# Opening of the first attention layer: projections as pairs of 64-row matmuls, and another order of norms, mask copies and late copies

## The chip, the cores and the metric

The kernel runs on one core of one Trainium2 chip. A core has TensorE (PE; matmuls into PSUM, eight banks of 128 x 512 f32), VectorE (DVE), ScalarE (ACT), GpSimd (POOL) and SyncE (SP); DMAs are issued from the queues of SP, ACT and POOL. The metric is the device time of the whole program in microseconds, the median of several executions.

## The reference

Four layers over `x` of 2048 tokens by 576, each with a layer norm ahead and a residual: attention, gated MLP, attention, gated MLP.

```python
def _A_ref(x, wqkv, wo):            # H = 32 heads of Dh = 18, window W = 8, dilation 2
    q, k, v = split(x @ wqkv)
    idx = pos[:, None] - 2 * arange(8)[None, :]     # eight tokens back, two apart
    logits = einsum('bhsd,bhswd->bhsw', q, k[idx]) * Dh ** -0.5   # masked where idx < 0
    return einsum('bhsw,bhswd->bhsd', softmax(logits), v[idx]) @ wo

def _B_ref(x, w_in, w_sp, b_sp, w_out):
    z = gelu(x @ w_in)
    z1, z2 = z[..., :Fh], layernorm(z[..., Fh:])
    return (z1 * (w_sp @ z2 + b_sp)) @ w_out
x = x + _A_ref(layernorm(x)); x = x + _B_ref(layernorm(x)); and both once more
```

## The kernel before

**Data.** In the attention layers the tokens are held with even ones first and odd ones behind (`rows_of`), so that the window is eight neighbours. `xnT` holds the normed input transposed: five chunks of 128 rows by 2048 columns (tokens). The model width of 576 is four full chunks and one of 64 rows; chunk 4 has 64 real rows in partitions 0 to 63. Each 128-token tile `xn` is 640 wide before it is transposed, so partitions 64 to 127 of chunk 4 hold its columns 576 to 639. In layer 0 of the kernel before these are zeros, written once by POOL (L151); in the later layers they are a second copy of columns 512 to 575, and the MLP layers use them.

**Weights.** `wqk` holds chunks 0 to 3 of the Q and K weights, `wqk4` chunk 4. In layer 0 `wqk4` has the weights in partitions 0 to 63 and zeros in 64 to 127 (`zero_right`, L340, on VectorE), so a matmul over all 128 rows of chunk 4 takes the 64 real ones.

**First attention layer (`layer_A`, `li == 0`).** An order written by hand holds for all five engines: each executes its instructions in the order of the program text, and waits where an operand, a buffer or a bank is not ready.

- *Norms.* For each tile of 128 tokens: `B_` (two statistics, L715), `G_` (aggregation, L718), `S_` is both; `R_` adds the epsilon on VectorE (L727) and takes the power -0.5 on POOL (L728); `A_` writes the normed tile (L735, VectorE). The first four tiles are transposed by TensorE (`T_pe`, L742) and copied by ScalarE (L745); the later ones by DMA transposes issued on SP (`T_`, L306). Four buffers of `xn` rotate.
- *V.* `VW(t, hh)` (L451): five matmuls of 288 columns for one query tile (17 tiles of 120 tokens with a halo of 8) and half of the heads, copied out of PSUM into `v_ext` by VectorE or ScalarE (`evac`).
- *Q and K projections.* `PG(d, qk, cc)` (matmuls at L462): one unit is 128 output columns (`d` 0 to 4; `qk` 1 is K, 0 is Q; `d` 4 has the last 64 columns of both in one unit) by 512 tokens (`cc`), five matmuls into one bank, then one copy into a staging tile. When a staging tile of `d` is full, DMAs move its heads' rows into `QK` (L78), on POOL's and SP's queues by turns. The first half (`cc` 0 and 1, 18 units) stands in the opening; six units of `cc` 2 and two more stand ahead of the steps (`pre`), the rest in the steps.
- *Window mask.* The window is added through extra rows of Q and K: `QK` holds 18 rows of data and 14 rows of a fixed pattern for each head. `build_window_rows` makes the pattern: `rows[2]` (VectorE, and two DMAs on SP) and `rows[3]` (POOL, four small instructions and a DMA, L179 to L182 and L78) write one period to DRAM, `load_pat` reads it into `win_pat` with four DMAs on SP, and `fill_window_rows` (L201, L204, VectorE) copies it over a half of `QK`, head groups 0 to 3 and then 4 to 7. The moves of a `d` into `QK` come after the copy over the same groups.
- *Banks.* One tile `X0` of three banks, tag Y with two banks and tag PT with three. `PT_tile` takes the next of the list `ring` ("Y", "Y", "PT", "PT", "PT").
- *Steps.* 34 steps follow, two for each query tile: logits of step s+1 (`L_mm`, L536), exponentials on ScalarE (`EXP`, L545), products with V (`PV`, L559) and what the table `at` puts into the step: projections, V units, transposes of the output `O_T` (L595, copied to `oT` by `evac`), output projection `WO` (L629). `pe_turn` lists the tiles whose output TensorE transposes, among the last 13 and 14 (of 17).

**64-row pairs.** The MLP layers split the rows of a contraction over two tiles of the array of 64 rows by 128 columns, which work side by side on different banks. `mm_phase` (L234) issues, for each chunk, a matmul of each of two outputs on different halves of the rows; then, in a second phase, each output takes the other half of the rows. Between the phases an engine writes a one-element token (`turn_on`), so that the two row tiles take turns on a bank. `pair` keeps two such pairs in flight.

The order in the opening of the kernel before, after the first four tiles:

```python
            S_(4, 5)
            R_(4, 2)
            A_(4, 5)
            T_(4, 5)
            S_(6, 7)
            R_(6, 2)
            rows[3](nc.gpsimd)
            A_(6, 7)
            T_(6, 7)
            S_(8)
            self.load_pat(nc.sync)
            S_(9, 10, 11)
            R_(8, 4)
            S_(12)
            A_(8, 9, 10, 11)
            T_(8, 9, 10, 11)
            self.fill_window_rows(QK, 0)
            S_(13, 14, 15)
```

The 18 units follow, `d` by `d` within `cc`, all copied out by ScalarE, with `R_(12, 4)` on POOL's queue behind the moves of `d` 0 to 2; then V tiles 4 to 7, `A_` and `T_` of tiles 12 to 15, `pre`, V tile 8 and the steps.

## Time and profile before

| | us |
|---|---|
| median of 3 runs | 1155.64 (1155.06 to 1156.4) |
| the profiled execution, its own time | 1155.03 |
| its span | 1153.3 |
| TensorE busy | 1144.1 |
| VectorE, ScalarE, POOL busy | 536.6, 373.3, 259.8 |
| granted TensorE clock, mean | 0.999 |

The first attention layer takes the first 123 us of the span, and the part that the change touches most lies between 1 and 50 us.

How to read the lines: a timeline row is the start in us, the length in us, the engine, the line of the kernel, the operation, output<-inputs, the number of instructions merged, and in brackets the idle time ahead with what ended it; "128*128 128x512" is the stationary and the moving operand of a matmul. SPq and POOLq are the queues on which DMAs are issued; the length there is that of issuing, not of landing. A row of a DMA group ends with its size and the time from issue to landing. A row of a table of windows has the window, its length, the busy time and the number of instructions of PE, PEld, DVE, ACT and POOL, the granted clock, the DMA engines' share and GB/s. The groups of one line give the shortest, the middle and the longest duration in ns.

### The profile page before, as it was taken

What the parts mean: (1) busy time and instruction counts of PE and PEld (TensorE: products, weight loads), DVE (VectorE), ACT (ScalarE), POOL (GpSimd) and SP (SyncE); (2) the same over time, 40 slices, a digit from 0 to 9 for tenths busy, and PEclk for the clock granted to TensorE, in tenths of its full rate; (3) what the DMA queues carried; (4) which work ended last, traced back from release to release, by engine and by line L of the source; (5) the groups of instructions that cost most, each with busy time, mean ns of one, the idle gap of its engine ahead of it and who ended that gap; (6) DMA issues with size and microseconds to landing.
All of it is one profiled execution on the core that took longest, in us unless ns stands there. A gap on an engine that the chain in (4) does not pass through costs nothing.

```text
span 1153.3 us, 29700 instructions
## 1 busy us (share of the span) xinstructions
PE 1144.1 (99%) x12935; PEld 613.6 (53%) x12954; DVE 536.6 (47%) x1189; ACT 373.3 (32%) x669; POOL 259.8 (23%) x387
## 2 busy tenths in 40 slices
PE   9999999999999999999999999999999999999998
PEld 5567554444444444457755774444444444444676
DVE  8788887222233222234476889843322223222311
ACT  5589565011111111102247876641111111011000
POOL 3689655000000000001153776530000000000000
PEclk9999999999999999999999999999999999999999
DMA  8867697000000000049455868930000000000322
GB/s 193 182 162 194 131 204 148 18 13 13 13 1 13 13 13 2 1 140 224 109 110 110 165 167 171 237 73 1 13 13 13 13 12 1 13 2 27 103 74 58
DMA packets 176701, 91.10 MB, mean 79 GB/s; under 512 B 128116, under 2 KB 169748, under 8 KB 176570
## 3 DMA queue, kind: packets, MB, share of 16 engines
q1 hardware_dynamic: 164090, 70.58, 28.0%
q0 software_dynamic: 5888, 12.72, 4.3%
q10 hardware_dynamic: 6592, 5.90, 1.7%
q8 instruction: 101, 1.65, 0.6%
q14 instruction: 30, 0.25, 0.1%
HBM read 35.46 MB, written 14.69 MB: 43 GB/s over the span
## 4 chain that ended last, share of the span: by engine, by line
PE 96%; ACT 1%; DMA 1%; issue 1%; SPq 0%; DVE 0%; DVEq 0%; ACTq 0%
PE hh L234 79%; PE pp L462 6%; PE pv L451 3%; PE pw L629 3%; PE O_ps L559 2%; PE L_ps L536 2%; ACT P_sb L545 1%; DMA wqk_sb<-in_A_wqkv_dram 1%; PE L_ps L462 1%; SPq L78 0%; PE hh L1191 0%; PE pt L595 0%; DVE x_new L632 0%; DVE ln_st L640 0%; ACT v_ext L445 0%
## 5 line engine op out<-in xcount | busy, mean ns | idle before, releaser
L234 PE MATMUL hh<-Wq,Z 64*128 64x512 bf16 x4608 | 505.8, 376 | 0.0
L234 PEld LDWEIGHTS <-Z 64*128 64x128 bf16 x6984 | 338.5, 94 | 311.4
L1095 DVE TENSOR_TENSOR g_tmp<-hh,ln_xn 128x512 f32<-128x512 f32 x144 | 92.8, 686 | 452.3 <-PE hh L234 452.3
L947 ACT COPY bank_turn<-ones 1x1 bf16<-1x1 bf16 x239 | 44.7, 187 | 538.6 <-PE hh L234 534.1
L78 POOL DMA_DIRECT2D wout<-in_B_w_out_dram x4 | 4.3, 1075 | 602.0 <-PE hh L234 602.0
L234 PE MATMUL hh<-wout,Z 64*128 64x288 bf16 x2232 | 137.0, 283 | 0.0
L545 ACT ACTIVATE P_sb<-L_ps 128x1440 bf16<-128x1440 f32 (+3 forms) x136 | 125.1, 972 | 21.8 <-PE L_ps L536 20.6
L234 PE MATMUL hh<-xnT,w 64*128 64x512 bf16 x1152 | 132.1, 376 | 0.0
L234 PE MATMUL hh<-win2a,xnT 64*128 64x512 bf16 (+1 forms) x960 | 118.6, 355 | 0.0
L234 PEld LDWEIGHTS <-xnT 64*128 64x128 bf16 x1440 | 69.6, 94 | 70.3 <-issue 0.5
L1020 DVE BATCH_NORM_STATS2 z_st<-zp 128x6 f32<-128x512 bf16 (+1 forms) x160 | 92.6, 623 | 11.1 <-ACT zp L1018 11.1
L1086 ACT ACTIVATE z1T<-hh 128x1024 bf16<-128x1024 f32 x72 | 73.7, 1024 | 62.2 <-PE hh L234 62.2
L1096 DVE TENSOR_TENSOR Z<-g_tmp,z1T 128x512 bf16<-128x512 f32 x144 | 92.4, 683 | 0.0
L234 PEld LDWEIGHTS <-w 64*128 64x128 bf16 x1152 | 55.8, 94 | 68.5
L1018 ACT ACTIVATE zp<-hh 128x1024 bf16<-128x1024 f32 (+1 forms) x96 | 76.1, 810 | 48.8 <-PE hh L234 48.7
L462 PE MATMUL pp<-xnT,wqk_sb 128*128 128x512 bf16 (+1 forms) x313 | 74.4, 379 | 1.0 <-DMA wqk_sb<-in_A_wqkv_dram 0.2
L234 PE MATMUL hh<-win2b,xnT 64*128 64x512 bf16 (+1 forms) x480 | 72.8, 355 | 0.0
L1160 DVE TENSOR_TENSOR x_new<-hh,xo 128x288 bf16<-128x288 f32 x64 | 26.3, 453 | 92.6 <-PE hh L234 84.7
L299 POOL TENSOR_SCALAR ln_xn<-x_new,ln_mv,ln_rstd 128x576 bf16<-128x576 bf16 x28 | 64.2, 2293 | 2.6
L78 POOL DMA_DIRECT2D QK<-stg x76 | 48.1, 636 | 35.6 <-DVE stg L443 22.5
L1044 POOL TENSOR_SCALAR Z<-zp,z_mv,z_rstd 128x256 bf16<-128x256 bf16 x32 | 51.2, 1599 | 3.5
L462 PEld LDWEIGHTS <-wqk_sb 128*128 128x128 bf16 (+1 forms) x360 | 32.0, 97 | 37.0 <-issue 1.9
(124 smaller groups left out, 755.2 us busy)
## 6 DMA issues: line engine op xcount, KB each, us to landing
xres<-x_new SPq DMA_DIRECT2D x44, 144.0 KB
wout<-in_B_w_out_dram POOLq DMA_DIRECT2D x4, 1296.0 KB, 7.5
xo<-xres SPq DMA_DIRECT2D x32, 144.0 KB
xn_rows<-ln_xn SPq DMA_DIRECT2D x28, 160.0 KB
w<-in_B_w_in_dram SPq DMA_DIRECT2D x16, 256.0 KB
QK<-stg POOLq DMA_DIRECT2D x51, 72.0 KB, 4.4
QK<-stg SPq DMA_DIRECT2D x37, 72.0 KB
xo<-in_A_x_dram SPq DMA_DIRECT2D x6, 288.0 KB
```

The lines of the kernel that those rows point to most:

```text
L78: return eng.dma_start(out=out, in_=in_)
L234: ins = self.nc.tensor.matmul(outs[a_], lhsT=lhs(a_, c, r0), rhs=rhs(a_, c, r0), start=start and k_ == 0, stop=stop and k_ == len(chunks) ...
L299: e.tensor_scalar(out=xn[:nrows, 0:D], in0=x_t[:nrows, :], scalar1=mv[:nrows, 0:1], scalar2=rstd[:nrows, 0:1], op0=ALU.subtract, op1=ALU.mult)
L462: nc.tensor.matmul(pp, lhsT=w, rhs=self.xnT[r0:r1, c, cc * 512:(cc + 1) * 512], start=start, stop=stop, tile_position=(r0, 0))
L545: nc.scalar.activation(out=P_bufs[2 * jp + s % 2][:nk, :, :, 0:nq], in_=Lv[:nk, :, :, 0:nq], func=ACT.Exp, scale=scale)
L947: self.turn_on = lambda tok: nc.scalar.copy(out=tok, in_=self.ones[0:1, 0:1])
L1018: nc.scalar.activation(out=zp[:, w0:w0 + n], in_=pz, func=ACT.Gelu_apprx_tanh)
L1020: nc.vector.bn_stats(out=st[:, x // 512, :], in_=zp[:, x:x + min(512, w0 + n - x)])
L1044: eng.tensor_scalar(out=Z[:, b0:b1, i, :], in0=zv[:, b0:b1, :], scalar1=mv[:, 0:1], scalar2=rstd[:, 0:1], op0=ALU.subtract, op1=ALU.mult)
L1086: lambda ht, z1T=z1T, q2=q2: nc.scalar.activation(out=z1T[:, q2 * 512:(q2 + 2) * 512], in_=ht[:].rearrange("p a b -> p (a b)"), func=ACT.G ...
L1095: nc.vector.tensor_tensor(out=tmp[:], in0=pg[:, a_, :], in1=bsp[:, qs], op=ALU.add)
L1096: nc.vector.tensor_tensor(out=uT(jj)[:, sub, qs], in0=tmp[:], in1=z1Ts[jj, sub][:, qs], op=ALU.mult)
```

## The change

- The 18 projection units become nine pairs, each run by `mm_phase` in two phases of 64-row matmuls: chunks 0 to 3, then the other half of the rows and chunk 4 of both. The first phase of a pair comes ahead of the second phase of the pair before it. ScalarE writes the token. Pairs are K of `d` 0 and 1, K of 2 and 3, Q of both for tokens 0 to 511, then K and Q of each `d` for tokens 512 to 1023, then `d` 4 for both token ranges. Banks go through `X0`, Y and PT in a cycle of four pairs.
- For the 64-row phases chunk 4 needs real data in partitions 64 to 127: `A_` copies columns 512 to 575 again behind each norm (VectorE), POOL's zero padding is gone, and `wqk4` is loaded into partitions 64 to 127 by three DMAs on POOL. VectorE no longer zeroes them at the start but after the last pair.
- Order: `rows[3]` moves ahead of the statistics of tile 4; `S_(6)` and `S_(8)` move ahead of the norms of tiles 4 and 6; the first half of the mask copy moves ahead of the statistics of tiles 9 to 12, the second behind the norms of tiles 8 to 11; the transposes of tiles 8 to 11 move between the pairs; `R_(12, 4)` moves behind the pairs.
- V tile 4 is computed around the last pair, tiles 5 to 8 behind the pairs, tile 9 ahead of the steps; it was tiles 4 to 7 and 8. Steps 10 and 14 lose a V unit each.
- The copies of the transposed output of tiles 13 and 14, and the V copies of steps 27 and 30, go from ScalarE to VectorE.

```diff
-        for xb in self.xn_bufs:
-            nc.gpsimd.memset(xb[:, D:640], 0.0)
...
-    def fill_window_rows(self, QK, half):
+    def fill_window_rows(self, QK, half, g0s=(0, 4)):
...
+    def load_wqk4_again(self, eng):
+        for c0, n, w0 in self.WQK_PARTS:
+            self.dma(self.right["wqk4"][64:128, w0:w0 + n], self.A_wqkv[512:576, c0:c0 + n], eng=eng)
...
-                evac(oT[:, :, c0:c0 + n], pt[:, :, a:a + n], t in pe_turn and t < NT - 4)
+                evac(oT[:, :, c0:c0 + n], pt[:, :, a:a + n], t in pe_turn)
...
-            self.zero_right()
+            self.zero_right(False)
...
+                    nc.vector.tensor_copy(out=xn[:, D:640], in_=xn[:, 512:D])
...
             VW(2, 1, False)
+            rows[3](nc.gpsimd)
+            self.load_wqk4_again(nc.gpsimd)
             VW(3, 0, False)
...
             S_(4, 5)
             R_(4, 2)
+            S_(6)
             A_(4, 5)
             T_(4, 5)
-            S_(6, 7)
+            S_(7)
             R_(6, 2)
-            rows[3](nc.gpsimd)
+            S_(8)
             A_(6, 7)
             T_(6, 7)
-            S_(8)
             self.load_pat(nc.sync)
+            self.fill_window_rows(QK, 0, (0,))
             S_(9, 10, 11)
             R_(8, 4)
             S_(12)
             A_(8, 9, 10, 11)
-            T_(8, 9, 10, 11)
-            self.fill_window_rows(QK, 0)
+            self.fill_window_rows(QK, 0, (4,))
             S_(13, 14, 15)
-            order = [(d, cc) for cc in range(2) for d in range(5)]
-            for k_, (d, cc) in enumerate(order):
-                for qk in ((1, 0) if d < 4 else (0,)):
-                    PG(d, qk, cc, False, (nc.gpsimd, nc.sync) if d in (0, 3, 4) else q2)
-                if k_ == 7:
-                    R_(12, 4)
-            nvw0, nvw = 4, 9
+
+            self.turn_on = lambda tok: nc.scalar.copy(out=tok, in_=self.ones[0:1, 0:1])
+
+            def PG_first(units, outs):
+                def lhs(a_, c, r0):
+                    d, qk, cc = units[a_]
+                    w0 = d * P + (640 if qk else 0)
+                    return wqk[r0:r0 + 64, c, w0:w0 + P] if c < 4 else wqk4[r0:r0 + 64, w0:w0 + P]
+
+                def rhs(a_, c, r0):
+                    cc = units[a_][2]
+                    return self.xnT[r0:r0 + 64, c, cc * 512:(cc + 1) * 512]
+                turn = self.mm_phase(outs, lhs, rhs, [0, 1, 2, 3], 0, True, False)
+
+                def second():
+                    self.mm_phase(outs, lhs, rhs, [0, 1, 2, 3, 4], 1, False, True, turn)
+                    for u, o in zip(units, outs):
+                        PG(*u, False, (nc.gpsimd, nc.sync) if u[0] in (0, 3, 4) else q2, pp=o)
+                return second
+
+            def pair_banks(p):
+                if p % 4 == 0:
+                    return [X0[:, 0, :], X0[:, 1, :]]
+                one = [X0[:, 2, :]] if p % 4 == 2 else []
+                self.ring = ["Y"] if p % 4 == 1 else ["PT"]
+                return one + [self.PT_tile([P, 512], f32, "pp")[:, :] for _ in range(2 - len(one))]
+
+            order = [((d, qk, 0), (d + 1, qk, 0)) for qk in (1, 0) for d in (0, 2)]
+            order += [((d, 1, 1), (d, 0, 1)) for d in range(4)] + [((4, 0, 0), (4, 0, 1))]
+            second = None
+            for p, units in enumerate(order):
+                then = PG_first(units, pair_banks(p))
+                if second is not None:
+                    second()
+                    if p in (5, 6):
+                        T_(2 * p - 2, 2 * p - 1)
+                second = then
+            self.ring = ["Y", "Y", "PT", "PT", "PT"]
+            R_(12, 4)
+            VW(4, 0, True)
+            second()
+            nc.vector.memset(wqk4[64:128, :], 0.0)
+            VW(4, 1, False)
+            nvw0, nvw = 5, 10
...
-        vsteps = ([x for x in range(PG_END - 4, NST - 3) if x % 4] if li == 0 else
+        vsteps = ([x for x in range(PG_END - 3, NST - 3) if x % 4 and x != PG_END] if li == 0 else
...
-            at(vsteps[k_], VW, t, hh, vsteps[k_] >= PG_END - 4 and k_ % 2 == 0)
+            at(vsteps[k_], VW, t, hh, (k_ % 2 == 0 or k_ > len(vws) - 4) if li == 0 else vsteps[k_] >= PG_END - 4 and k_ % 2 == 0)
```

More of the change, by code (lines that the diff above doesn't have):

```diff
@@ L195, in make_ident @@
                                 base=0, pattern=[[-1, P]], channel_multiplier=1)
-    def fill_window_rows(self, QK, half):
+    def fill_window_rows(self, QK, half, g0s=(0, 4)):
         nc, n = self.nc, self.cfg.S // 2
-        for g0 in (0, 4):
+        for g0 in g0s:
             for a in range(2):
@@ L342, in zero_right @@
         nc.vector.memset(R["wo"][64:128, 4, :], 0.0)
+    WQK_PARTS = ((D, 512, D + 64), (0, D, 0), (D + 512, 64, D))
+    def load_wqk4_again(self, eng):
+        for c0, n, w0 in self.WQK_PARTS:
+            self.dma(self.right["wqk4"][64:128, w0:w0 + n], self.A_wqkv[512:576, c0:c0 + n], eng=eng)
     def load_wqk(self, eng, twice=False):
         R = self.right
-        for c0, n, w0 in ((D, 512, D + 64), (0, D, 0), (D + 512, 64, D)):
+        for c0, n, w0 in self.WQK_PARTS:
             self.dma(R["wqk"][:, :, w0:w0 + n], self.A_wqkv[0:512, c0:c0 + n].rearrange("(c p) n -> p c n", p=P), eng=eng)
```

## The prediction

> **What bounds the kernel now.** I read the page's busy shares and chain first, then the timeline of each engine over the first 50 us, where the change lies.
>
> ```profile
> PE 1144.1 (99%) x12935; PEld 613.6 (53%) x12954; DVE 536.6 (47%) x1189; ACT 373.3 (32%) x669; POOL 259.8 (23%) x387
> PE 96%; ACT 1%; DMA 1%; issue 1%; SPq 0%; DVE 0%; DVEq 0%; ACTq 0%
> ```
>
> TensorE carries 96% of the chain: whatever shortens its instructions is a gain, and whatever makes it wait is a loss at full price. TensorE's timeline around the change:
>
> ```profile
> 13.39 1.24 PE L462 MATMUL pp<-xnT,wqk_sb 128*128 128x512 bf16 x4
> 14.82 18.52 PE L462 MATMUL pp<-xnT,wqk_sb 128*128 128x512 bf16 x84 [0.19 <-DMA wqk_sb<-in_A_wqkv_dram]
> 33.18 5.06 PE L451 MATMUL pv<-wv_sb,xnT 128*128 128x288 bf16 x40
> 38.08 4.48 PE L462 MATMUL pp<-xnT,wqk_sb 128*128 128x512 bf16 x19
> 47.15 1.39 PE L451 MATMUL pv<-wv_sb,xnT 128*128 128x288 bf16 x10
> 48.47 0.63 PE L536 MATMUL L_ps<-QK 32*128 32x128 bf16 x16
> ```
>
> The 18 projection units of the first half run from 13.39, eight V units from 33.18 (4.90/8 = 0.61 each), the `pre` projections from 38.08, V tile 8 from 47.15, and the second logits block, L(1), from 48.47. I carry everything to L(1); behind it TensorE is full, so a shift there is a shift of the end.
>
> **The pairs.** ScalarE's timeline (it copies each unit out) gives a unit's price, and the second layer, which already works in 64-row pairs, a pair's:
>
> ```profile
> 14.67 0.59 ACT L445 CAST stg<-pp 128x512 bf16<-128x512 f32 x1 [0.68 <-PE pp L462]
> 16.11 0.59 ACT L445 CAST stg<-pp 128x512 bf16<-128x512 f32 x1 [0.85 <-PE pp L462]
> 33.38 0.59 ACT L445 CAST win2a<-pp 128x512 bf16<-128x512 f32 x1 [0.49 <-PE pp L462]
> ...
> 124.20 0.81 PE L234 MATMUL hh<-win2a,xnT 64*128 64x512 bf16 x6
> 125.06 0.81 PE L234 MATMUL hh<-win2a,xnT 64*128 64x512 bf16 x6
> ```
>
> A unit of five matmuls takes (33.38-16.11)/16 = 1.08. Eight 64-row matmuls take 0.86 (124.20 to 125.06), so ten 1.08: a pair's phases cost 0.86+1.08 = 1.94 where two units cost 2.16. Nine pairs save 1.9. The weight wait (16.11-14.67 is 1.44, not 1.08) saves 0.36 more, as the first two pairs need K columns only. The nine turn tokens are small ScalarE copies two phases ahead of their reader, the two copies a pair (1.2 in 1.94) keep ScalarE ahead: nothing. So 2.3 on paper.
>
> **The first wait: transposes.** The phase order is first(0), first(1), second(0), first(2), ... so first(4), which reads tokens 512 to 1023, comes 4x0.86+3x1.08 = 6.7 after 13.4, at 20.1, where before those columns were wanted 9x1.08+0.36 after, at 23.5. Queues that feed it:
>
> ```profile
> 11.25 0.82 DVE L715 BATCH_NORM_STATS2 ln_st<-x_in 128x6 f32<-128x288 bf16 x2 [0.90 <-DMA x_in<-in_A_x_dram]
> 14.26 0.77 DVE L735 TENSOR_SCALAR ln_xn<-x_in,lnx_mv,lnx_rstd 128x576 bf16<-128x576 bf16 x2 [0.81 <-POOL lnx_rstd L728]
> 30.44 0.18 DVE L204 COPY QK<-win_pat 128x64 bf16<-128x64 bf16 x1
> 30.54 0.81 DVE L715 BATCH_NORM_STATS2 ln_st<-x_in 128x6 f32<-128x288 bf16 x2
> 33.48 0.17 DVE L727 TENSOR_SCALAR lnx_rstd<-lnx_mv 128x4 f32<-128x4 f32 x1
> 13.52 0.70 POOL L728 TENSOR_TENSOR lnx_rstd<-lnx_rstd,neg_half 128x2 f32<-128x2 f32 x1 [3.86 <-DVE lnx_rstd L727]
> 18.85 0.76 POOL L78 DMA_DIRECT2D win_period<-win_first  x1 [0.31 <-POOL win_first L182]
> win_period<-win_first POOLq DMA_DIRECT2D x1, 0.4 KB, 3.5
> 19.72 1.50 SPq L306 DMA_TRANSPOSE xnT<-ln_xn  x1
> 22.50:23.00 0.50, 0.50 (x4) 0.20 (x2) 0.49 (x3) 0.41 (x1) 0.23 (x1) 1.00 0.00 0
> ```
>
> A tile's statistics cost VectorE (33.48-30.54)/3 = 0.98. The new duplicate copy of 64 columns has its nearest row in the 128x64 mask copy, 0.18; it waits for the norm ahead of it, so 0.2 a tile (0.1 if it overlapped). The three loads put `wqk4` into partitions 64 to 127, which second(0) wants in its last chunk, at 13.4+2x0.86+0.9 = 16.0; the nearest landing from POOL is the rows part's 3.5 after its issue, and the first load is issued at about 11.9, so 15.4: hidden, and if up to 1.9 late still inside the wait below. VectorE from 11.25: two statistics to 13.3, one more to 14.4 while POOL takes the root. POOL first has the moved row part and the three added weight loads (0.76 and about 3x0.6, in an idle stretch of 3.86), ready at about 14.4 too. Two norms with copies 1.1, two more statistics 2.0, two norms 1.1: tile 7 is ready at 18.7, hardly earlier than before, for the two root waits of 0.81 that are now covered pay for the copies. Its transpose goes out behind tile 6's at 19.5, ends at 20.8, and lands 1.2 later (before: issued until 21.22, and the queue moved nothing from 22.5). So first(4) waits from 20.1 to 22.0, and the pairs end at 22.0+5x0.86+6x1.08 = 32.8 (33.4 with V(4,0) between), against 33.18. The 2.3 has shrunk to 0.4. The start before that (0.54 of weight zeroing leaves VectorE, up to 0.6 of copies for three tiles comes) may move 0.3 either way and is inside this wait.
>
> **The second wait: VectorE at the mask.**
>
> ```profile
> 1.10 0.54 DVE L340 MEMSET wqk_sb<- 64x576 uint32 x1 [0.18 <-issue]
> 22.43 1.60 SPq L78 DMA_DIRECT2D win_pat<-win_period  x4
> 22.51 0.17 DVE L727 TENSOR_SCALAR lnx_rstd<-lnx_mv 128x4 f32<-128x4 f32 x1
> 23.84 1.45 DVE L735 TENSOR_SCALAR ln_xn<-oT,lnx_mv,lnx_rstd 128x576 bf16<-128x576 bf16 x4 [0.20 <-POOL lnx_rstd L728]
> 25.57 2.36 DVE L201 COPY QK<-win_pat 128x4096 bf16<-128x4096 bf16 x2 [0.28 <-issue]
> 28.05 2.35 DVE L201 COPY QK<-win_pat 128x4096 bf16<-128x4096 bf16 x2
> 33.99 0.46 DVE L443 CAST v_ext<-pv 128x288 bf16<-128x288 f32 x1 [0.34 <-PE pv L451]
> 39.71 1.45 DVE L735 TENSOR_SCALAR ln_xn<-x_in,lnx_mv,lnx_rstd 128x576 bf16<-128x576 bf16 x4 [1.58 <-POOL lnx_rstd L728]
> 41.07 2.48 DVE L443 CAST stg<-pp 128x512 bf16<-128x512 f32 x4
> ```
>
> The mask load stays behind the four transposes on SP, so it goes out at 20.9 instead of 22.43. Its first reader now stands ahead of the statistics of tiles 9 to 12, and VectorE works in order. The reader came 3.14 after the issue before, without a clear wait: 24.0 at the latest, 23.6 at the earliest by how far that was slack; I take 23.8. VectorE, idle since 18.7, then runs: first mask half 2.5 (26.3), three statistics 2.9 (29.2), root until first norm 1.33 (30.55), four norms with copies 1.45+0.8 (32.8), second mask half 2.5 (35.3), three statistics 2.9 (38.2), the add, and only now V(4,0)'s copy, 38.4 to 38.9. Before, that copy was just in time at 33.99. TensorE, at 33.4, still has banks for V(4,1), V(5,0), V(5,1), V(6,0): 35.9. V(6,1) takes V(4,0)'s bank (the ring has two Y and three PT) and waits to 38.9: 3.0 lost. Five V units more: 42.0, where the old order with nine tiles done would stand at 38.08+1.23 = 39.3. The zeroing (0.54) is on VectorE behind that copy, hidden by the banks. The transposes of tiles 8 to 11 follow their norms from 31.1, 1.3 each with some moves into QK between them on SP, and are down by about 40, before the `pre` projections want them; those of tiles 12 to 15 are wanted only in step 1, behind 52.9. The removed zero padding on POOL (four small fills) was ahead of nothing late: nothing.
>
> **The third: POOL's moves and the last root.**
>
> ```profile
> 28.89 9.73 POOL L78 DMA_DIRECT2D QK<-stg  x15 [5.08 <-ACT stg L445]
> 38.64 1.04 POOL L728 TENSOR_TENSOR lnx_rstd<-lnx_rstd,neg_half 128x4 f32<-128x4 f32 x1
> 39.63 2.45 POOL L78 DMA_DIRECT2D QK<-win2a  x4
> L78 POOL DMA_DIRECT2D QK<-stg x15: 522/590/1627, 28.9 to 38.1; - x15
> ```
>
> POOL's moves into QK stand behind the root of tiles 8 to 11, now done at 30.6. Four fit before the second mask half; the move that met a mask copy took 1.63 against 0.59, ending with it, so I hold POOL until 35.3 (at least 0, at most 2.5). Fifteen more at 0.59 end at 44.2, as the last root now stands behind the moves of d=3 as well: root 45.2, four norms with copies 47.5, and the copies of the `pre` projections, queued behind them on VectorE, begin there instead of at 41.07. TensorE does five (and L(0), 0.34) to 47.8, waits 0.4 for a bank, then for the fifth copy (50.6): 51.7 for the eighth, 1.2 for V tile 9, L(1) at 52.9. That is 4.4 behind 48.47, of which 1.2 is V tile 9, taken out of steps 10 and 14: +3.2. The second half's mask copies end at about 55, later than PV(0) wants VectorE; three banks take most of that: +0.3.
>
> **Late copies.**
>
> ```profile
> 109.84 0.67 ACT L445 COPY oT<-pt 128x600 bf16<-128x600 bf16 x1
> ```
>
> Two such copies (t=13, 14) and two V copies leave ScalarE, where the exponentials set the pace in the last steps. Each lies between exponentials and opens 0.3 to 0.4; VectorE there is nearly full. I take -0.5 (0 to -0.7).
>
> **Sum.** +3.2+0.3-0.5 = +3.0 on the profiled execution's 1155.03, that is 1158.0; the median of the runs is 0.6 higher, so 1158.6. Copies at 0.1, the mask at 23.6 and POOL not held make it +1.3; a mask at 24.4 and slower landings +4.7: own range 1156.9 to 1160.3.
>
> **Rivals.** *VectorE's delay is absorbed* (not slower). Place: V(4,0)'s bank and the last root. It decides if the mask reaches VectorE by 20.8, 3.0 sooner, for then V(6,1) finds its bank and POOL starts before 28. For it: the rows part, which the mask load needs, now leaves POOL at about 11.1 instead of 18.85. Against: SP is busy with transposes until 20.8 and the load takes 1.6 to issue alone. Then -0.4 from the pairs and -0.5 late: 1154.7, and down to 1152.8 if also the tile-7 wait is short.
>
> *TensorE's clock drops in the 3 us wait.* The trace shows both halves of it:
>
> ```profile
> 1.36 4.45 PE L699 MATMUL warm<-ident 128*128 128x128 bf16 x46 [1.36 <-POOL ident L194]
> 1145.18 4.58 PE L1191 MATMUL hh<-wout,Z 128*128 128x288 bf16 x36
> 1151.00:1152.00 1.00, 0.00 (x0) 0.00 (x0) 0.00 (x0) 0.00 (x0) 0.00 (x0) 0.93 0.51 148
> ```
>
> After the last matmul (1149.76) the granted clock is halved within 1151 to 1152 (0.93 mean), some 2.1 us later; and the 46 warming matmuls took 97 ns each, against 54 for a quarter of a 512-column one: 2.0 us lost to a cold start. With 0.4 of slack at the bank behind it, +1.5: 1160.1. The Trainium skill ("TensorE: Matmul & The Clock Gate", Part 1) asks for an idle window of about 3.4 us before the clock halves, which would spare a wait of 3.0 and leave the sum as it is; the end of this trace shows it sooner.
>
> *Pairs that don't run side by side* (the change would not do what it says) would take twice 1.94, nine times +1.94 = +17.5 us, 1176; the second layer's rows speak against it.
>
> **Chances.** Forecast 0.48 (a quarter of it under +0.2%), absorbed 0.29 (0.12 of it faster by over 0.2%), clock 0.20, rest 0.03. 0.2%, 2.3 us, is about what a measurement here can tell. Faster 0.12, same 0.30, slower 0.58. Leaving out the far ends of the absorbed and clock cases, the range is 1154.0 to 1161.0.
>
> **What would show it.** In the changed kernel's trace: 64-row matmuls from about 13.5, a TensorE wait of 1 to 2 us near 20 ended by the transposes; VectorE idle for some 5 us until its first mask copy near 24; a V matmul near 36 waiting for VectorE; a root on POOL near 44; L(1) near 52.9; fewer waits for ScalarE after 109. The prediction is wrong if the first mask copy starts before 21, or if V(4,0)'s copy comes before 36.

## The result and the profile after

The changed kernel takes 1165.82 us (median of six runs, 1161.58 to 1169.08), the kernel before in the same comparison 1155.58: a ratio of 1.0089, interval 1.0078 to 1.01. The forecast was 1158.6, slower, with 1161.0 as the upper end: the direction came true, the size lies outside the range by 5 us.

The profiled execution took 1166.36 us, its span 1164.6 (before: 1153.3). Its busy shares and its chain, from the page:

```profile
PE 1148.0 (99%) x13026; PEld 614.9 (53%) x13026; DVE 541.6 (47%) x1209; ACT 372.4 (32%) x674; POOL 261.1 (22%) x386
PE 95%; ACT 2%; DMA 1%; DVE 1%; issue 1%; POOL 0%; DVEq 0%; ACTq 0%
```

TensorE's share of the chain falls from 96% to 95%, about 1% of 1164 us, and ScalarE and VectorE come in instead: TensorE waits. Where it waits is in its timeline over the opening (start, length, instructions, and in brackets the idle time ahead with what ended it):

```profile
13.89 1.04 PE L232 MATMUL L_ps<-xnT,wqk_sb 64*128 64x512 bf16 x8
14.77 1.03 PE L232 MATMUL pp<-xnT,wqk_sb 64*128 64x512 bf16 x8
17.81 0.39 PE L232 MATMUL L_ps<-xnT,wqk_sb 64*128 64x512 bf16 x2 [1.16 <-DMA wqk_sb<-in_A_wqkv_dram]
19.37 0.37 PE L232 MATMUL L_ps<-xnT,wqk_sb 64*128 64x512 bf16 x1 [1.17 <-ACT stg L449]
25.79 1.04 PE L232 MATMUL L_ps<-xnT,wqk_sb 64*128 64x512 bf16 x8 [0.67 <-ACT stg L449]
31.02 0.37 PE L232 MATMUL L_ps<-xnT,wqk_sb 64*128 64x512 bf16 x1 [1.17 <-ACT stg L449]
35.76 1.04 PE L232 MATMUL L_ps<-xnT,wqk_sb 64*128 64x512 bf16 x8 [0.67 <-ACT stg L449]
39.71 5.69 PE L455 MATMUL pv<-wv_sb,xnT 128*128 128x288 bf16 x45
49.74 6.16 PE L466 MATMUL pp<-xnT,wqk_sb 128*128 128x512 bf16 x20 [4.34 <-issue]
61.81 0.40 PE L540 MATMUL L_ps<-QK 32*128 32x128 bf16 x16
```

L(1) starts at 61.81, before at 48.47: 13.3 later, of which 1.23 is V tile 9, now ahead of it. The span is 11.3 longer, so from L(1) on it is 2.0 shorter, V tile 9's 1.23 and another 0.8. The waits of the rows are 1.16 for `wqk4`, 3.68 at four of the pairs for ScalarE's copies, and 4.34 ahead of `pre`; on top the last row but one shows 6.16 us for `pre`'s first 20 matmuls, which took 4.48 before.

VectorE, POOL and SP around it:

```profile
24.60 2.36 DVE L199 COPY QK<-win_pat 128x4096 bf16<-128x4096 bf16 x2 [5.20 <-DMA win_pat<-win_period]
31.33 0.43 DVE L739 TENSOR_SCALAR ln_xn<-oT,lnx_mv,lnx_rstd 128x576 bf16<-128x576 bf16 x1 [0.16 <-POOL lnx_rstd L732]
39.04 0.46 DVE L447 CAST v_ext<-pv 128x288 bf16<-128x288 f32 x1
49.67 0.43 DVE L739 TENSOR_SCALAR ln_xn<-x_in,lnx_mv,lnx_rstd 128x576 bf16<-128x576 bf16 x1 [0.71 <-DMA xnT<-ln_xn]
```

```profile
46.14 1.04 POOL L732 TENSOR_TENSOR lnx_rstd<-lnx_rstd,neg_half 128x4 f32<-128x4 f32 x1
```

```profile
31.00 3.52 SPq L78 DMA_DIRECT2D QK<-stg  x4
34.62 2.55 SPq L304 DMA_TRANSPOSE xnT<-ln_xn  x2
37.27 2.70 SPq L78 DMA_DIRECT2D QK<-stg  x3
40.08 3.31 SPq L304 DMA_TRANSPOSE xnT<-ln_xn  x2
45.25 6.65 SPq L78 DMA_DIRECT2D QK<-win2a  x8
```

VectorE idles 5.20 us until the mask's rows arrive, norms tiles 8 to 11 from 31.33 (before: 23.84), and copies V(4,0) at 39.04. SP issues the transposes of tiles 10 and 11 from 40.08 to 43.4, between moves into QK. The norm at 49.67, tile 15's, goes into tile 11's buffer and has waited for that transpose; `pre`, which reads tile 11's columns, starts 0.07 later. So tile 11 landed near 49.6, and it is what ended the opening here.

### The profile page after: what moved, and what is told of

Its sections match the earlier page's. It is cut to its first block, busy times and chain, and to the rows that moved or that the text cites. A ratio compares the mean times of both kernels' runs of the same rounds, so it can differ in the third digit from the quotient of the medians.

```text
span 1164.6 us, 29879 instructions
## 1 busy us (share of the span) xinstructions
PE 1148.0 (99%) x13026; PEld 614.9 (53%) x13026; DVE 541.6 (47%) x1209; ACT 372.4 (32%) x674; POOL 261.1 (22%) x386
## 4 chain that ended last, share of the span: by engine, by line
PE 95%; ACT 2%; DMA 1%; DVE 1%; issue 1%; POOL 0%; DVEq 0%; ACTq 0%
PE hh L232 78%; PE pp L466 4%; PE pw L633 3%; PE pv L455 2%; PE O_ps L563 2%; PE L_ps L540 2%; ACT P_sb L549 1%; PE pp L232 1%; DMA xnT<-ln_xn 1%; PE L_ps L232 1%; PE L_ps L466 1%; DMA wqk_sb<-in_A_wqkv_dram 0%; PE hh L1235 0%; ACT stg L449 0%; DVE ln_st L719 0%
## 5 line engine op out<-in xcount | busy, mean ns | idle before, releaser
L1064 DVE BATCH_NORM_STATS2 z_st<-zp 128x6 f32<-128x512 bf16 (+1 forms) x160 | 92.7, 623 | 11.4 <-ACT zp L1062 11.4
L466 PE MATMUL pp<-xnT,wqk_sb 128*128 128x512 bf16 (+1 forms) x240 | 57.5, 387 | 4.3 <-issue 4.3
L455 PE MATMUL pv<-wv_sb,xnT 128*128 128x288 bf16 x340 | 49.4, 285 | 0.8 <-ACT xnT L750 0.8
```

What stands on the lines that cost most here:

```text
L455: nc.tensor.matmul(pv[:nk, 0:288], lhsT=self.xnT[:, c, k0_(t):k0_(t) + nk], rhs=wv_sb[:, c, hh * 288:(hh + 1) * 288], start=(c == 0), stop ...
L466: nc.tensor.matmul(pp, lhsT=w, rhs=self.xnT[r0:r1, c, cc * 512:(cc + 1) * 512], start=start, stop=stop, tile_position=(r0, 0))
L1064: nc.vector.bn_stats(out=st[:, x // 512, :], in_=zp[:, x:x + min(512, w0 + n - x)])
```

## The experiments

The times are medians. The ratio is to the kernel before, run on the same chip beside each; it is taken over all runs and not from the two medians, so that a kernel with a few short runs (e4, e12) has a ratio below that of its medians. L(1) is its start in the profiled run.

| run | us | ratio, interval | L(1) |
|---|---|---|---|
| the change | 1165.82 | 1.0089 (1.0078 to 1.0100) | 61.81 |
| e1 banks | 1165.76 | 1.0088 (1.0075 to 1.0101) | 61.12 |
| e2 transposes | 1165.27 | 1.0083 (1.0070 to 1.0096) | 62.23 |
| e3 wqk4 | 1163.70 | 1.0075 (1.0063 to 1.0087) | 58.32 |
| e4 mask later | 1167.26 | 1.0095 (1.0078 to 1.0112) | 57.01 |
| e5 = e1+e2 | 1163.92 | 1.0078 (1.0065 to 1.0091) | 57.98 |
| e6 = e5 + mask later | 1157.36 | 1.0023 (1.0014 to 1.0032) | 52.69 |
| e7 = e6 + wqk4 | 1157.93 | 1.0030 (1.0019 to 1.0041) | 53.72 |
| e8 late copies alone | 1154.51 | 0.9997 (0.9988 to 1.0006) | 48.30 |
| e9 = e6 + root early | 1155.99 | 1.0010 (1.0001 to 1.0019) | 51.29 |
| e10 = e9 + three more | 1162.04 | 1.0062 (1.0048 to 1.0076) | 55.56 |
| e11 before, root late | 1162.59 | 1.0065 (1.0052 to 1.0077) | 55.66 |
| e12 before, mask early | 1166.25 | 1.0091 (1.0074 to 1.0108) | 56.90 |
| e13 = e10 mended | 1155.12 | 1.0001 (0.9992 to 1.0009) | 49.16 |
| e14 = e9, banks as changed | 1159.55 | 1.0036 (1.0023 to 1.0049) | 54.02 |
| e15 change, root early | 1166.12 | 1.0094 (1.0078 to 1.0109) | 61.68 |

A profile is one execution, and the runs of a kernel with long waits scatter by several us (e4: 1161.64, the profiled one, to 1168.62), so L(1) and the median need not agree; the last section shows what scatters. The theory ahead of the experiments was that the losses lie beneath one another, so that taking one away uncovers the next; its rival, that each wait is a loss of its own.

### One wait at a time: e1 to e4

e1, other banks for the pairs:

```diff
-                if p % 4 == 0:
+                if p % 3 == 0:
                     return [X0[:, 0, :], X0[:, 1, :]]
-                one = [X0[:, 2, :]] if p % 4 == 2 else []
-                self.ring = ["Y"] if p % 4 == 1 else ["PT"]
-                return one + [self.PT_tile([P, 512], f32, "pp")[:, :] for _ in range(2 - len(one))]
+                self.ring = ["Y"] if p % 3 == 1 else ["PT"]
+                return [self.PT_tile([P, 512], f32, "pp")[:, :] for _ in range(2)]
```

> The changed kernel with other banks for the pairs: a cycle of three places (X0 with both its banks, Y, PT) in place of every second pair in X0. Four waits of TensorE for ScalarE's copies in the changed kernel's trace sum to 3.7 us (1.17, 0.67, 1.17, 0.67). Theory A (TensorE is held by three things one after the other: these waits, a halved clock behind them, the transposition of tile 11): the waits go, the moves and with them the transposition of tile 11 are issued up to 3.7 us earlier, and L(1) starts at 58 to 59 in place of 61.8; what stays is a wait for tile 11 of about 4 us ahead of `pre`. Time 3 to 4 us less than the changed kernel. Rival B (the chain that was predicted: VectorE at the mask, then V tile 4's copy at 39): L(1) stays at 61 to 62, as V's first units wait for their bank till 39 instead.

TensorE's timeline in e1, from the end of the pairs:

```profile
40.08 3.22 PE L455 MATMUL pv<-wv_sb,xnT 128*128 128x288 bf16 x25 [1.60 <-DVE v_ext L447]
48.00 7.21 PE L466 MATMUL pp<-xnT,wqk_sb 128*128 128x512 bf16 x20 [4.70 <-issue]
```

The four waits at the pairs are gone. One of 1.20 stands at pair 4 (23.41); the profile puts it down to ScalarE, but the two banks of Y that this pair writes had been copied out by 21.4, and e5, e6 and e9 wait there for tile 7's transpose, so it is probably that. Further on comes the forecast's wait of a V unit for VectorE, 1.60 us, then 4.70 for tile 11, and `pre`'s first 20 matmuls take 7.21, not 4.48. L(1) gains 0.7 and the time nothing: nearer to B in L(1), but for A's reason, a transpose that comes when it comes.

e2, the transposes of tiles 8 to 11 ahead of the moves:

```diff
             A_(8, 9, 10, 11)
+            T_(8, 9, 10, 11)
             self.fill_window_rows(QK, 0, (4,))
...
-                    if p in (5, 6):
-                        T_(2 * p - 2, 2 * p - 1)
```

> The changed kernel with the transpositions of tiles 8 to 11 issued right behind these tiles' norms, ahead of the moves, as the kernel before has them. Theory A: tile 11 is there before 42, the wait of 4.34 us ahead of `pre` goes, and with it the halved clock behind it (1.7 us): L(1) at about 55.8 in place of 61.8, the time 6 us less than the changed kernel; the waits for ScalarE's copies stay. Rival B (the end of the opening hangs on VectorE and POOL: the root at 46.1 and the norms from 47.2): `pre` starts no earlier than 47.7, L(1) at 58 to 60. Rival C (the four transpositions stand ahead of the moves on SP and make them late): `pre` starts at 45.5, but L(1) waits for a move into QK.

```profile
44.65 4.48 PE L466 MATMUL pp<-xnT,wqk_sb 128*128 128x512 bf16 x20 [0.35 <-DMA QK<-stg]
53.38 0.58 PE L540 MATMUL L_ps<-QK 32*128 32x128 bf16 x13 [4.09 <-DVE stg L447]
53.90 7.18 PE L466 MATMUL pp<-xnT,wqk_sb 128*128 128x512 bf16 x20
```

`pre` starts 5.1 earlier and loses nothing to the clock, as A has it; then L(0) waits 4.09 us, for VectorE's copies of `pre`, which waited for staging buffers that SP's moves had not yet emptied, and the next 20 matmuls take 7.18. That is C: SP cannot have the transposes early and the moves early, as both start behind norms that end at 34.

e3, the second load of `wqk4` by ScalarE, right behind the ones of V:

```diff
+            self.load_wqk4_again(nc.scalar)
             rows[0]()
...
-            self.load_wqk4_again(nc.gpsimd)
```

> The changed kernel with the second load of wqk4 issued by ScalarE at the start in place of POOL at 12. Theory A: the wait of 1.16 us at the second phase of pair 0 goes, and the clock falls to half less or not at all behind the next wait (1.17 us): L(1) 1.2 to 2.5 us earlier than 61.8. Rival B (the next wait takes it up): L(1) within 0.3 of 61.8.

The wait of 1.16 goes, and of the two stretches at half clock of the change's profile only the second is left. L(1) is 3.5 earlier (1.2 for the load, 1.7 for the clock, 0.4 less of the wait for tile 11) and the median 2.1 lower: A, by a little more than it said, but within the scatter of the change's six runs.

e4, both mask halves behind the norms of tiles 8 to 11:

```diff
-            self.fill_window_rows(QK, 0, (0,))
             S_(9, 10, 11)
...
-            self.fill_window_rows(QK, 0, (4,))
+            self.fill_window_rows(QK, 0)
```

> The changed kernel with all four mask copies of the first half behind the norms of tiles 8 to 11, so that VectorE waits for the mask's rows with nothing behind it that is wanted early. Theory A (VectorE's wait lies beneath TensorE's own delays): L(1) within 0.5 us of 61.8, the time as the changed kernel's. Rival B (the prediction's second wait, 3.0 us at V tile 4's bank, is part of the loss): L(1) at about 59, 3 us less.

```profile
46.62 4.48 PE L466 MATMUL pp<-xnT,wqk_sb 128*128 128x512 bf16 x20 [3.07 <-issue]
```

The median, 1167.26, shows no gain, as A said. A's L(1) did not come true: the profiled run, the shortest of six, whose clock stayed full, has it at 57.01 and not at 61.8; of the 4.8, 3.4 is the clock. Even there `pre` still waits 3.07 us for tile 11: its transpose stands behind moves on SP as before, whenever the norm is done. So no single undoing brings the loss back; e15 below is a fifth.

### Several at once: e5 to e7

> The changed kernel with both the three places for the pairs and the early transpositions of tiles 8 to 11. In the run with the early transpositions alone SP issued them from 32.4 to 38.8, the moves into QK from 38.8 to 54.8, and L(0) waited for them to 53.4. Theory A (SP's queue sets the end of the opening: tiles 8 to 11 are normalised only at 32 to 34, behind the mask, and whatever of transpositions and moves stands behind the other is late): freeing TensorE of the waits for banks moves neither, L(0) stays at 52 to 54 and L(1) at 58.5 to 62. Rival B (TensorE's own waits are the loss, and both are gone now): L(1) at 53 to 55, the time about 1158.

> The same and the whole mask behind the norms of tiles 8 to 11. Theory A: these norms come at 23.6 to 25.9 as in the run with the late mask alone, SP issues the four transpositions at 24 to 30 and the moves from 30 to 45, as in the kernel before (24.3 to 29.5, 29.6 to 43.8), L(0) starts at 44 to 46 and L(1) at 50 to 52; with 1104.6 us behind L(1) that is 1154.6 to 1156.6. Rival B (the VectorE wait at the mask was not part of it): as the run without the mask's move, within 1 us.

> The same and the second load of wqk4 issued by ScalarE at the start: all four edits. Theory A: SP's moves, not TensorE, end last, so that the 1.2 us of the wait for wqk4 bring 0 to 0.5: L(1) at 49.5 to 52, the time 1154 to 1156.5, the kernel before's within 0.2%. Rival B (TensorE ends last): 1.2 us less than without this edit.

e5 to e6 is the mask's place and nothing else, and it is worth 6.6 us: with the norms at 24, SP issues transposes and moves within 1 us of the kernel before. The edits are those of e1, e2, e4 and e3, added one by one. e5 itself lies between its two theories: L(0) waits 2.63 us for copies, till 50.55, not 52 to 54. e6 misses A's L(1) by 0.7 and its time by 0.8. In e7 both theories miss: L(1) is 1.0 later than in e6 and the time 0.6 higher. It shows why `wqk4` is worth nothing by then, in TensorE's timeline:

```profile
23.08 1.04 PE L232 MATMUL pp<-xnT,wqk_sb 64*128 64x512 bf16 x8 [2.31 <-DMA xnT<-ln_xn]
23.95 1.96 PE L232 MATMUL L_ps<-xnT,wqk_sb 64*128 64x512 bf16 x10
```

Pair 4, the first to read tokens 512 to 1023, is reached 1.7 earlier and waits 2.31 for tile 7's transpose (e6: 1.05), and the clock falls behind it: ten matmuls take 1.96, not 1.24. This is the prediction's first wait, which the losses above it had hidden; the two waits of e6, 1.26 for `wqk4` and 1.05 for tile 7, add up to the one of e7.

### The late copies: e8

```diff
-                evac(oT[:, :, c0:c0 + n], pt[:, :, a:a + n], t in pe_turn and t < NT - 4)
+                evac(oT[:, :, c0:c0 + n], pt[:, :, a:a + n], t in pe_turn)
...
-            at(vsteps[k_], VW, t, hh, vsteps[k_] >= PG_END - 4 and k_ % 2 == 0)
+            at(vsteps[k_], VW, t, hh, (k_ % 2 == 0 or k_ > len(vws) - 4) if li == 0 else vsteps[k_] >= PG_END - 4 and k_ % 2 == 0)
```

> The kernel before with the change's late copies alone: five copies behind step 26 moved from ScalarE to VectorE. The prediction put these at 0.5 us less (0 to 0.7); from L(1) on the changed kernel's trace is about 0.8 us shorter than before's once V tile 9 is counted. Expected: 0.3 to 0.8 us less than the kernel before; rival: nothing, as no wait of TensorE ends with ScalarE there.

0.3 us less in the median, with an interval that holds both nothing and a gain of 1: not settled. TensorE's waits for the exponentials between 100 and 125 add up to 0.9 us before, 0.6 in e8 and 0.2 in the change.

### One cause at a time, in the kernel before: e11 and e12

e11, the root of tiles 12 to 15 behind all moves of the units:

```diff
-                if k_ == 7:
-                    R_(12, 4)
+            R_(12, 4)
             nvw0, nvw = 4, 9
```

> The kernel before, with nothing changed but the last root's place on POOL: behind the moves of all units of the first half. Theory A: root at about 44 in place of 38.6, norms of tiles 12 to 15 at 45, the copies of `pre` behind them at 47 in place of 41.1, so that L(0) and L(1) are 4 us late: 3 to 5 us more than the kernel before. Rival B (the price that the prediction put on its third step, 0.3 to 0.7 us): 0.2 to 1 us more.

L(0) in the kernel before, then TensorE's timeline and VectorE's in e11:

```profile
42.49 0.40 PE L536 MATMUL L_ps<-QK 32*128 32x128 bf16 x16
```

```profile
41.96 0.23 PE L536 MATMUL L_ps<-QK 32*128 32x128 bf16 x3
47.33 0.58 PE L536 MATMUL L_ps<-QK 32*128 32x128 bf16 x13 [5.14 <-DVE stg L443]
47.85 6.66 PE L462 MATMUL pp<-xnT,wqk_sb 128*128 128x512 bf16 x19
```

```profile
44.63 1.45 DVE L735 TENSOR_SCALAR ln_xn<-x_in,lnx_mv,lnx_rstd 128x576 bf16<-128x576 bf16 x4 [7.04 <-POOL lnx_rstd L728]
46.00 2.48 DVE L443 CAST stg<-pp 128x512 bf16<-128x512 f32 x4
```

The norms come at 44.63 instead of 39.71 and the copies of `pre` behind them at 46.00 instead of 41.07. Three matmuls of L(0) run, the fourth waits 5.14 us: it writes a bank of Y, and until its copy a unit of `pre` has that bank. Then `pre`'s next 19 take 6.66 instead of 4.49. 5.14 and 2.17 make 7.3 of the 7.7 by which the way from L(0) to L(1) is longer (13.70 against 5.98); in the median the cost is 7.7 too. A was right on the mechanism and short of its size, most of all by the clock, which it had left out; B was far too low.

e12, the first mask half ahead of the statistics of tiles 9 to 11:

```diff
             self.load_pat(nc.sync)
+            self.fill_window_rows(QK, 0, (0,))
             S_(9, 10, 11)
...
-            self.fill_window_rows(QK, 0)
+            self.fill_window_rows(QK, 0, (4,))
```

> The kernel before, with nothing changed but the first two of the four mask copies moved ahead of the statistics of tiles 9 to 11, as the change has them; its units, banks, transpositions and loads stay. Theory A (VectorE's wait for the mask's rows makes tiles 8 to 11 late, and with them everything behind them on SP): norms at 32 to 34 in place of 24 to 26, transpositions to 38, moves to 53, L(0) at about 50 in place of 42.5: 6 to 10 us more than the kernel before. Rival B (the prediction's second step: only V's copies on VectorE are late): 2 to 4 us more.

SP in the kernel before, then VectorE, SP and TensorE in e12:

```profile
24.30 5.19 SPq L306 DMA_TRANSPOSE xnT<-ln_xn  x4
29.59 7.73 SPq L78 DMA_DIRECT2D QK<-stg  x9
```

```profile
23.34 2.36 DVE L201 COPY QK<-win_pat 128x4096 bf16<-128x4096 bf16 x2 [4.73 <-DMA win_pat<-win_period]
30.10 1.45 DVE L735 TENSOR_SCALAR ln_xn<-oT,lnx_mv,lnx_rstd 128x576 bf16<-128x576 bf16 x4 [0.20 <-POOL lnx_rstd L728]
```

```profile
30.55 6.34 SPq L306 DMA_TRANSPOSE xnT<-ln_xn  x4
36.98 8.23 SPq L78 DMA_DIRECT2D QK<-stg  x9
45.32 6.41 SPq L78 DMA_DIRECT2D QK<-win2a  x8
```

```profile
37.47 2.00 PE L451 MATMUL pv<-wv_sb,xnT 128*128 128x288 bf16 x15 [1.51 <-DVE v_ext L443]
41.63 4.48 PE L462 MATMUL pp<-xnT,wqk_sb 128*128 128x512 bf16 x19 [2.16 <-DMA xnT<-ln_xn]
48.25 0.40 PE L536 MATMUL L_ps<-QK 32*128 32x128 bf16 x11 [1.98 <-DVE stg L443]
49.41 0.23 PE L536 MATMUL L_ps<-QK 32*128 32x128 bf16 x2 [0.75 <-DMA QK<-stg]
49.57 6.18 PE L462 MATMUL pp<-xnT,wqk_sb 128*128 128x512 bf16 x19
```

One line moved, and the norms of tiles 8 to 11 are 6.3 later than before, SP's transposes too, and its 17 moves 7.4. TensorE pays in four waits, 1.51 for V's bank (the prediction's wait), 2.16 for tile 11, 1.98 and 0.75 for copies and a move, and 1.7 in clock: 8.1 of the 8.4 by which L(1) is late. The median is 11.4 above the kernel before, the whole loss of the change, with none of its pairs. A, and 1.4 over its range; the profiled run, at 1163.3, was the shortest of five.

### What the pairs are worth: e9, e10, e13, e14, e15

e9, the root where the kernel before has it:

```diff
+                if p == 7:
+                    R_(12, 4)
                 second = then
             self.ring = ["Y", "Y", "PT", "PT", "PT"]
-            R_(12, 4)
```

> The run with banks, transpositions and mask mended, and the last root (tiles 12 to 15) ahead of the moves of the last two pairs on POOL, where the kernel before has it. In that run the root ended at 43.2, the norms of tiles 12 to 15 at 45.5, and the first copies of `pre`, behind them on VectorE, came at 45.9; L(0) had its 13 last matmuls at 46.65. Theory A (the root behind POOL's moves, the prediction's third step, is what holds L(0) now): the root at about 40, the copies at about 43, L(0) at 45.9, L(1) 0.5 to 0.8 earlier than 52.69, the time 1156.5 to 1157. Rival B (SP's and POOL's moves hold it: staging buffers come free at 45 to 46 whatever the root does): within 0.2.

L(0)'s wait is gone, L(1) is 1.4 earlier and the time 1.4 lower: A, and more than it said. In the profiled runs 0.56 of it is there before `pre` starts (40.89 against 41.45), where the root has no part, and 0.84 behind. 1155.99 is 0.1% above the kernel before.

e10 adds three edits, tile 7 by TensorE among them:

```diff
-            T_(6, 7)
+            T_(6)
...
                 then = PG_first(units, pair_banks(p))
+                if p == 3:
+                    T_pe(7)
...
-            self.ring = ["Y", "Y", "PT", "PT", "PT"]
+            self.ring, self.ring_rr = ["Y", "Y", "PT", "PT", "PT"], 4
```

> The same, with wqk4's second load by ScalarE, tile 7 transposed by TensorE (five matmuls and a copy of ScalarE, as for tiles 0 to 3) between the first phase of pair 3 and the second of pair 2, and a free bank for V's first unit: all of the waits of TensorE in the last run's opening (1.26, 1.05, 0.67) are gone on paper, and 0.45 of transposing comes in. Theory A (TensorE ends last): L(1) at about 49.5, the time 1154.0 to 1154.5, 0 to 0.8 below the kernel before. Rival B (the moves on SP and POOL end last): L(0) no earlier than 45, L(1) at 51 to 52, the time 1155.5 to 1156.5, no better than the kernel before.

Tile 11's norm goes into tile 7's buffer, and the edit lets it do so before tile 7 is read: this run transposes tile 11's rows in tile 7's place, so that it computes something else, and TensorE waits 5.56 us for them. Its time says nothing on either theory. e13 gives tile 7 a buffer of its own:

```diff
-                    xns[i] = xn = self.xn_bufs[self.xn_rr % len(self.xn_bufs)]
-                    self.xn_rr += 1
+                    if i == 7:
+                        xn = sb.tile([P, 640], bf16, name="xn_seven", tag="xn_seven", bufs=1)
+                    else:
+                        xn = self.xn_bufs[self.xn_rr % len(self.xn_bufs)]
+                        self.xn_rr += 1
+                    xns[i] = xn
```

> The run with banks, transpositions, mask and root mended (1155.99 us; L(0) at 45.30, L(1) at 51.29), with wqk4's second load by ScalarE, tile 7 transposed by TensorE from a buffer of its own, and a free bank for V's first unit. Theory A (TensorE ends last): its waits of 0.94, 1.03 and 0.67 go, 0.45 of transposing comes in, L(1) at about 49.1 and the time at 1153.8, 1 us below the kernel before: the pairs' gain is there. Rival B (the moves on SP and POOL end last: in that run `pre`'s copies waited for a staging buffer to 43.46): L(0) no earlier than 44.8 and L(1) than 50.8, the time 1155.3 to 1156, no better than the kernel before.

```profile
13.95 1.04 PE L232 MATMUL L_ps<-xnT,wqk_sb 64*128 64x512 bf16 x8
19.66 0.45 PE L752 MATMUL pt<-ident,xn_seven 128*128 128x128 bf16 x5
32.85 5.69 PE L455 MATMUL pv<-wv_sb,xnT 128*128 128x288 bf16 x45
38.38 4.48 PE L466 MATMUL pp<-xnT,wqk_sb 128*128 128x512 bf16 x20
42.79 0.79 PE L540 MATMUL L_ps<-QK 32*128 32x128 bf16 x16
49.16 0.40 PE L540 MATMUL L_ps<-QK 32*128 32x128 bf16 x16
```

No wait is left on these rows, L(1) is where A had it, and the profiled run took 1154.09. The pairs run from 13.95 to 32.85; less 0.45 for the transposes and 0.7 for V(4,0), which lies among them, that is 17.8, where the 18 units took 19.8: the 2 us of the prediction's first term are there. (In e8, e11 and e12, whose profiled runs have no wait for weights, the 18 units take 19.4; against these the pairs save 1.7.) But L(1) is only 0.5 ahead of the kernel before's 48.47 plus 1.23, mostly since the pairs start 0.56 later, the transposes cost 0.45 and L(0) takes 0.79 in place of 0.40; and the median of eleven runs, 1155.12, can't be told from the kernel before's. A for the opening, neither for the median; why ten of the eleven runs are 0.1 to 4 us longer than the profiled one stays open (the longest alone, at a mean clock of 0.998, has an evident reason).

e14, e9 with the change's own banks:

```diff
-                if p % 3 == 0:
+                if p % 4 == 0:
                     return [X0[:, 0, :], X0[:, 1, :]]
-                self.ring = ["Y"] if p % 3 == 1 else ["PT"]
+                one = [X0[:, 2, :]] if p % 4 == 2 else []
+                self.ring = ["Y"] if p % 4 == 1 else ["PT"]
```

> The same run (banks, transpositions, mask and root mended) but with the change's own banks for the pairs, every second pair in X0. Theory A (the four waits for ScalarE's copies are then on the path, less the wait for tile 7 that they cover): 3.7 less 1.0, so 2.5 to 3 us more than 1155.99, and more where the clock falls. Rival B (the moves end last, and cover the waits): 0 to 1 us more.

3.6 us more than e9, with the profiled run at a full clock (1.000): the four waits of 1.17, 0.67, 1.17 and 0.67 come back to the hundredth, and tile 7's wait of 1.03 goes beneath them. The two profiled runs differ by 2.7, as A had it; in the medians its price was up to 1 us short.

e15, the change with e9's place for the root alone:

> The changed kernel with the last root alone put ahead of the moves of the last two pairs. Theory A (the losses lie beneath one another; tile 11's transposition sets the start of `pre`): L(1) within 0.5 us of 61.8, no gain beyond the noise of the changed kernel's times. Rival B (the root's 7.7 us are a part of the change's 10.9): 4 to 8 us less than the changed kernel.

L(1) at 61.68 and no gain: A. What costs 7.7 us alone in the kernel before is worth nothing inside the change, since tile 11 comes later than the root.

## Why the prediction was wrong, by its steps

Of the signs that it named, VectorE's idle 5 us until a mask copy near 24 is there; TensorE's wait for tile 7 near 20 and V's wait for VectorE near 36 are not, and the root and L(1) are later than it said.

- *The pairs.* The price, 0.86 and 1.08, came true (13.89 to 14.77 is 0.88), and so did the 2 us, in e13; the 0.36 for the weights is of one execution, for e8, e11 and e12 have no such wait. The "nothing" beside it failed: ScalarE's copies cost four waits, 3.7 us, and 3.6 in e14 against e9. The step counted ScalarE's time and not the order on X0: pair 2 writes X0's third bank, and waits at 19.37 for copies out of the first two; the order is kept for the tile as a whole.
- *`wqk4` by POOL.* Landing was put at 15.4, from one small DMA; the three were issued from 12.57 and the last had landed at 17.8, so TensorE waited 1.16 us. That such a delay lies "inside the wait below", for tile 7, is right where there is nothing else (1.26 and 1.05 in e6, 2.31 in e7 without the first). In the change the bank and the slower clock behind it carry TensorE past tile 7 anyway, and the 1.16 counts in full.
- *The first wait.* Tile 7 was put at 22.0. In the change it is hidden by the waits above; where these are gone it shows, 1.03 to 1.05 in e6 and e9, 2.31 in e7, till 22.9 to 23.5. Right in mechanism and about 1 us early; e13, where it is taken away with two smaller waits, has the pairs' gain.
- *The second wait.* This is the step that failed most. VectorE's times came true within 1 us (mask 24.60 for 23.8, norms 31.33 for 30.55, V(4,0)'s copy 39.04 for 38.4), and its price was looked for in V's bank, 3.0, which measured 1.5 to 1.6 where TensorE got there in time. The sentence that failed is that the transposes of tiles 8 to 11 "are down by about 40, before the `pre` projections want them". They landed at 49.6: 4.34 of waiting, and a stretch at half clock. The harm is done on SP, where the transposes and 17 moves share one queue. The mask's delay makes all of them late: e12 shows it alone at 11.4 us, e5 against e6 at 6.6. The transposes' new place behind moves makes tile 11 later still: with it undone (e2) `pre` hardly waits, with the mask's delay alone undone (e4) `pre` waits 3.07. The prediction named both and put the price of either on SP at nothing.
- *The third.* The root came at 46.1 for 44.2, by the chain as reckoned and 1.9 late. What failed is that TensorE "does five (and L(0), 0.34)" before late copies hold it, "0.4 for a bank" first: L(0) itself needs a bank of Y that `pre` holds, behind four units, and waits 5.14 in e11. In the change this lies beneath the second, which is why e15 gains nothing.
- *Late copies.* -0.5 was forecast; from L(1) on the span is 0.8 shorter, e8 shows -0.3 and can't tell it from nothing.
- *The rivals.* Absorption did not happen. The clock did fall, as that rival had it, near its price (1.5; measured 1.3 to 1.7 a time, and 2.2 to 2.7 where it lasted twice as long), but twice, and in other waits than the one it named; in the runs here it fell at nine of the eleven waits of over 2 us. It belonged in the sum, not among the rivals.

In numbers, L(1) was put 3.2 late and is 12.1 late, V tile 9 left out. The profile's own rows give the difference: start 0.5, `wqk4` 1.2, banks 3.7, tile 11 4.3, clock 3.4, less 1.9 and 0.4 for pairs and weights, 10.8 in all. About 1.0 of the other 1.3 is, as an estimate, what a wait costs beside its idle time: rows of eight matmuls last 1.04 and follow each other by 0.87, so 0.17 of overlap is lost at each of the six waits. 0.3 stays without a row. That the direction came true is in part luck: the delay of the mask and the root was seen, the paths by which it cost the most were not.

## What to carry to other kernels

An engine that waits in its queue delays what it would have done next, and the price is found by following those outputs through the queue that carries them away: a norm that is 6 us late here cost 11 us by way of SP, and the wait beside it 1.5. Where several chains end near the same place, a loss that is real alone (7.7 us) can be worth nothing undone (e15), so undo them all first and then put each back. And where waits of 2 us and more come in, up to 1.7 us of half clock for each, as these runs have it, belongs in the sum.

## What the runs showed of the hardware

The half-clock stretches have a fixed length. The change's windows of 0.5 us, first and last of eight, with the clock behind the five busy times:

```profile
19.50:20.00 0.50, 0.50 (x6) 0.21 (x4) 0.00 (x0) 0.00 (x0) 0.00 (x0) 0.68 0.36 49
20.00:20.50 0.50, 0.50 (x6) 0.26 (x4) 0.00 (x0) 0.00 (x0) 0.00 (x0) 0.50 0.92 196
22.50:23.00 0.50, 0.50 (x6) 0.26 (x4) 0.00 (x0) 0.00 (x0) 0.00 (x0) 0.50 0.26 26
23.00:23.50 0.50, 0.50 (x8) 0.27 (x6) 0.00 (x0) 0.33 (x1) 0.00 (x0) 0.91 0.19 36
```

0.32, six times 0.5, and 0.09 at half: 3.41 us, and by the same sum 3.41 again behind the wait ahead of `pre`, 3.42 in e12, and twice that, 6.8, in e1, e2 and e11. Each 3.41 us costs up to 1.7 us of TensorE's time. When a stretch begins is less fixed: behind one wait of 2.31 in e7, 1.3 us after work had begun again; at two of 1.2 in the change and in e15, but not in e4 and e14 with nearly the same two (0.93 or 1.13, and 1.17); and not behind 3.07 in e4 or 2.16 in e12. The places keep a raster, though: by windows of 0.1 us the clock falls at 19.68 and 50.40 in the change and at 18.84 and 49.56 in e15, each time 30.72 apart, which is nine times 3.413. So a wait's place on the raster counts and not its length alone. The share of the raster's window in which TensorE was busy does not decide alone either: 0 to 0.46 ahead of a fall, and 0.38 in e12 (39.57 to 42.98) without one.

The Trainium skill ("TensorE: Matmul & The Clock Gate", Part 1) has a free-running window of 3413 ns, which fits the length, the raster and the scatter; its rule of thumb that an idle window of about 3.4 us is needed is not what these runs show. It fits with this that the shortest run of the change, 1161.58, has a mean clock of 1.000 and the longest, 1169.08, one of 0.994 (between them the order is not strict: 1165.98 at 0.999, 1165.66 at 0.997), while eleven runs of the kernel before, all at 1.000, lie between 1154.53 and 1157.22.

A transpose issued among moves lands late: tile 11's was issued by 43.4 in the change and landed 6.2 us later (in e12 by 36.9, and 4.7 later), while the DMA engines' share was 1.14 (38 to 44) and 1.00 (44 to 50); the prediction had taken 1.2 from a queue that moved nothing else. That the moves are the cause was not tested alone.
